# A searched instruction order, engine choice and PSUM bank table for a two-layer SSM and MLP kernel

## The chip, the cores and the metric

The kernel runs as one program on one core of a Trainium2 chip. The core has a matmul engine (TensorE, PE in the profile, with its weight loads shown as PEld), a vector engine (VectorE, DVE), a scalar engine (ScalarE, ACT), a general engine (GpSimd, POOL) and a queue that issues most of the DMA transfers (SyncE, SP). Each of the five works through a list of its own, in order, and waits for the others by semaphores. The metric is device microseconds (us) of one execution, as the median of several; lower is better.

## The reference

An input of 2048 rows of 512 is passed twice through a pair of layers, with residual sums:

```python
x = A_q
x = x + _A_ref(_layernorm(x), A_k, A_v, A_shift_k, A_ssm_k, A_ssm_D)
x = x + _B_ref(_layernorm(x), B_w1, B_b1, B_w2, B_b2)
x = x + _A_ref(_layernorm(x), A_k, A_v, A_shift_k, A_ssm_k, A_ssm_D)
x = x + _B_ref(_layernorm(x), B_w1, B_b1, B_w2, B_b2)
```

`_A_ref(q, k, v, ...)` shifts k by a filter of four taps, multiplies it by v (`kv`), convolves `kv` along the 2048 rows with a filter of 2048 taps per channel (by FFT in the reference), adds `kv * ssm_D` and multiplies the sum y by the normed q. `_B_ref` is a layer norm, a 512 to 1376 matmul with bias and GELU, and a 1376 to 512 matmul with bias. Since k, v and the filters are the same in both passes, y is the same in both, and the kernel computes it once.

## The kernel before

The long convolution is done as a transform in matmuls, in two halves of 1024 rows. The source marks every operation with a stage name (`P.tag`), and the text below uses these names; `_0` and `_1` are the halves:

- `ht`, `h1`, `h2`: the filter is transposed (L540), goes through a first stage of matmuls (L557, 8 tiles of 16 matmuls) and a second (L569, 8 tiles of 16). A tile `t` of the second stage reads two of the 16 pieces of a constant table, `tab_s2` (256 KB each, operations 16 to 31, loaded at L463). `swap` copies the result from SBUF to SBUF in 8 transfers (issued by SP, L453).
- `fir0` to `fir3`: k is transposed (L589), the four-tap filter is a group of 22 matmuls (L614), and DVE multiplies the result by v (L620). Each of these products reads all four pieces of v of its half.
- `x1`, `x2`: the same two stages for kv (L557, L569). In `x2_0` DVE multiplies each result tile by the filter's transform (16 products of 128x1024, line L468).
- `i1`, `i2`: the way back, L674 and L696. Its result is y.

All of these stages evacuate PSUM through one helper, `evac` (L473 when it is ACT, L474 when it is DVE). From `i2_0` on the first half's blocks run: for a block b the stages are `q`b (layer norm of x, then y times it, added to x: `y`b, line L468), `z`b (a second norm, its statistics by L810/L811 on DVE and three small operations L815, L817, L822 or L825 on POOL or DVE, then L835 on ACT or L836 on DVE), a transpose (L887 on PE for the first two, by DMA at L879 for the others), `m1` (L899, one PSUM tile for each of 11 chunks, GELU on ACT at L904) and `m2` (L933, added to x by DVE at L937). The second half's transform (`h2_1` with products on DVE at L767, `fir4` to `fir7`, `p2`, `x1_1`, `x2_1`, `sum`, `i1_1`, `i2_1`) is threaded through the first half's blocks on the same engines; `p2`, `x2_1` and `sum` are DVE operations of 128x2048 at L468.

Nothing of the order is written out in the program's text. `op()` records 1185 operations with what they read and write. `arrange()` then takes three tables. `SEQ` is a permutation of the 1185 numbers, and the list of each engine is `SEQ` cut down to the operations of that engine. `ENGS` holds a letter (a, v, p for ACT, DVE, POOL) for each operation that could run on more than one engine. `BANKS` holds a digit for each PSUM tile, the first of its one or two banks (there are eight); a tile waits until the last user of its banks is through. `sync()` derives the semaphore waits from these lists: `d_N` is the landing of DMA operation N, `s_scalar`, `s_vector` and so on are counts of an engine's finished operations.

```python
self.seq = [self.ops[i] for i in self.SEQ]
choice = iter(self.ENGS)
for t, b in zip(self.tiles, self.BANKS):
    t.base = int(b)
```

Of the kernel before, what the change touches and what calls it, by code (L numbers as in the profile page):

```python
# [36 lines left out]
class Prog:  # L37
# [7 lines left out]
        42, 0, 6, 43, 214, 1, 4, 33, 2, 5, 34, 41, 7, 3, 195, 9, 11, 10, 8, 196, 51, 14, 197, 45, 52, 12, 209, 46, 35,  # L45
        53, 13, 36, 48, 28, 54, 49, 47, 20, 55, 67, 15, 59, 68, 19, 388, 50, 65, 32, 39, 430, 63, 60, 23, 40, 22, 64,
        66, 17, 56, 44, 69, 21, 38, 431, 389, 57, 24, 70, 390, 71, 29, 58, 391, 61, 18, 432, 37, 16, 62, 97, 134, 103,
        215, 392, 27, 104, 433, 98, 101, 26, 99, 136, 102, 105, 393, 31, 106, 100, 111, 72, 25, 114, 30, 108, 115,
        135, 133, 109, 116, 110, 112, 131, 113, 121, 132, 107, 129, 127, 130, 122, 472, 77, 528, 78, 125, 526, 126,
        79, 128, 80, 85, 73, 75, 74, 76, 117, 86, 139, 118, 89, 140, 83, 90, 474, 84, 123, 91, 473, 119, 124, 92, 120,  # L50
        81, 87, 475, 82, 476, 161, 88, 477, 169, 162, 478, 302, 93, 165, 434, 170, 173, 166, 94, 96, 143, 174, 95,
        181, 144, 194, 137, 182, 167, 200, 189, 163, 199, 185, 190, 210, 138, 177, 198, 186, 171, 141, 204, 175, 193,
        157, 178, 201, 159, 164, 142, 191, 187, 158, 155, 179, 147, 301, 183, 156, 153, 294, 184, 148, 220, 188, 176,
        160, 211, 216, 386, 192, 208, 154, 205, 172, 218, 203, 180, 221, 202, 222, 168, 206, 219, 226, 223, 217, 228,
        283, 580, 227, 224, 435, 527, 229, 230, 225, 282, 582, 149, 231, 479, 145, 529, 150, 530, 286, 146, 232, 531,
        234, 233, 240, 212, 532, 482, 235, 394, 581, 436, 151, 241, 395, 290, 238, 437, 295, 152, 396, 236, 438, 287,
        239, 397, 254, 583, 439, 398, 248, 399, 237, 255, 292, 242, 400, 256, 440, 401, 441, 243, 284, 442, 402, 291,
        244, 257, 584, 403, 585, 443, 249, 410, 412, 586, 406, 207, 411, 250, 444, 213, 407, 420, 293, 445, 258, 414,
        424, 387, 413, 422, 425, 259, 408, 421, 452, 288, 466, 409, 480, 418, 453, 416, 467, 483, 448, 417, 481, 456,
        419, 404, 285, 484, 449, 260, 485, 405, 289, 454, 415, 458, 423, 487, 251, 455, 536, 486, 462, 488, 426, 252,  # L60
        489, 457, 490, 463, 261, 427, 533, 491, 262, 459, 450, 494, 446, 253, 428, 447, 537, 495, 460, 451, 464, 429,
        492, 263, 534, 245, 590, 264, 493, 468, 461, 265, 465, 587, 469, 246, 470, 538, 247, 296, 535, 268, 541, 496,
        269, 471, 502, 497, 267, 539, 500, 503, 514, 272, 588, 501, 540, 510, 591, 515, 266, 542, 508, 592, 511, 543,
        589, 512, 270, 509, 544, 634, 498, 513, 273, 516, 298, 499, 545, 506, 517, 297, 504, 546, 635, 518, 593, 505,
        547, 595, 507, 522, 548, 594, 300, 523, 549, 596, 636, 597, 598, 299, 303, 271, 637, 599, 275, 638, 602, 310,
        524, 603, 304, 311, 639, 519, 305, 600, 640, 306, 520, 644, 307, 601, 558, 570, 521, 641, 554, 525, 571, 552,
        559, 689, 566, 568, 567, 645, 550, 278, 555, 556, 564, 557, 279, 562, 569, 560, 563, 610, 551, 276, 604, 611,
        608, 565, 642, 561, 616, 690, 609, 691, 622, 617, 620, 646, 605, 692, 612, 274, 553, 693, 606, 613, 624, 607,
        643, 614, 625, 694, 649, 572, 623, 615, 277, 695, 621, 308, 314, 309, 281, 322, 315, 576, 647, 696, 573, 323,
        280, 699, 320, 697, 316, 321, 648, 700, 318, 698, 574, 701, 317, 650, 702, 577, 651, 652, 319, 575, 312, 704,  # L70
        653, 313, 626, 703, 705, 744, 706, 578, 707, 654, 336, 708, 579, 655, 618, 337, 656, 328, 745, 746, 630, 619,
        657, 338, 329, 324, 627, 709, 747, 330, 748, 711, 749, 631, 710, 325, 339, 750, 340, 712, 332, 326, 632, 333,
        668, 633, 672, 669, 676, 341, 331, 628, 673, 660, 334, 677, 664, 661, 344, 665, 629, 721, 662, 722, 342, 731,
        345, 352, 335, 674, 663, 715, 675, 670, 353, 343, 717, 729, 671, 348, 718, 346, 658, 349, 382, 727, 383, 347,
        725, 659, 385, 713, 716, 384, 733, 714, 350, 719, 732, 730, 723, 751, 678, 354, 666, 680, 667, 351, 679, 720,
        684, 726, 355, 754, 685, 734, 327, 686, 728, 724, 735, 687, 366, 752, 755, 368, 367, 753, 756, 358, 757, 360,
        359, 759, 681, 799, 361, 758, 682, 760, 800, 369, 801, 761, 762, 364, 858, 370, 365, 763, 802, 860, 356, 803,
        855, 764, 371, 362, 861, 862, 765, 804, 736, 363, 766, 856, 805, 767, 737, 357, 857, 863, 859, 683, 739, 864,
        806, 865, 738, 374, 809, 807, 372, 866, 376, 373, 810, 808, 375, 740, 811, 377, 812, 782, 876, 867, 814, 786,
        778, 813, 873, 868, 788, 877, 774, 779, 815, 878, 870, 816, 772, 874, 770, 817, 869, 789, 875, 741, 775, 871,  # L80
# [893 lines left out]
```

## Time and profile before

| | us |
|---|---|
| median of 3 runs (lowest, highest) | 237.92 (237.78, 238.18) |
| the profiled execution's own time | 237.62 |
| its span, first to last instruction | 235.8 |
| PE busy | 223.4 |
| DVE busy | 177.0 |
| ACT busy | 161.7 |
| POOL busy | 55.2 |

The page cuts the span into 40 slices of 5.9 us and gives the busy share of each in tenths. The chain of waits follows the work that ended last back from step to step. The timeline gives start, length, engine, line and, in brackets, idle time ahead of a row with what ended it. A row of the timeline that merges several instructions (x4) reaches from the start of the first to the end of the last. On ACT and DVE an instruction starts about 0.1 us before the one ahead of it has ended, so the step from start to start is a little shorter than the length of one.

### The profile page before, as it was taken

The page shows a single profiled execution, that of the slowest core. Times are in us where ns is not written, and L with a number is a line of the kernel's source. Part 1 is how long each engine was busy: PE and PEld are TensorE (multiplying, and loading weights), DVE is VectorE, ACT ScalarE, POOL GpSimd, SP SyncE. Part 2 cuts the span into 40 slices and gives each one's busy share as a digit, 9 for nine tenths or more (in the row PEclk, how much of TensorE's full clock was granted, in tenths as well). Part 3 has the DMA queues.
Part 4 walks back from the last instruction along what each step waited for, and adds up shares of the span by engine and source line. Part 5 has one row for each costly group of instructions (what it writes and reads, how often), then busy time and mean ns, then how long its engine had stood idle before and what let it go on. Part 6 is the DMA issues. An engine that isn't in the chain of part 4 may idle for free.

```text
span 235.8 us, 6520 instructions
## 1 busy us (share of the span) xinstructions
PE 223.4 (95%) x2765; PEld 146.6 (62%) x2765; DVE 177.0 (75%) x355; ACT 161.7 (69%) x259; POOL 55.2 (23%) x117
## 2 busy tenths in 40 slices
PE   6796887998999999999999999999999999999995
PEld 3785777875968588667967585644444444444453
DVE  0678989999999999989999899385379388705004
ACT  2962999998996789998987995998037403810910
POOL 1550020924222405344002831402020301100000
PEclk9999999999999999999999999999999999999999
DMA  6999879983976930022140203301300140071302
GB/s 210 301 375 386 311 208 282 264 288 70 174 119 177 198 79 0 3 48 45 31 151 6 45 3 69 67 0 22 67 0 4 22 111 0 0 134 47 133 0 92
DMA packets 41113, 26.77 MB, mean 114 GB/s; under 512 B 23702, under 2 KB 33788, under 8 KB 41084
## 3 DMA queue, kind: packets, MB, share of 16 engines
q1 hardware_dynamic: 40786, 26.20, 41.2%
q8 instruction: 22, 0.36, 0.7%
q10 hardware_dynamic: 298, 0.16, 0.3%
q14 instruction: 7, 0.06, 0.1%
HBM read 15.07 MB, written 2.10 MB: 73 GB/s over the span
## 4 chain that ended last, share of the span: by engine, by line
PE 77%; DVE 7%; ACT 6%; SPq 4%; DMA 4%; issue 1%; DVEq 0%
PE ps L899 33%; PE ps L933 32%; ACT ar L473 6%; PE ps L569 4%; DMA ar<-in_A_v_dram 4%; DVE ar L468 4%; SPq L453 3%; PE ps L674 2%; PE ps L696 2%; DVE ar L620 2%; PE ps L557 2%; DVE ar L474 2%; PE ps L922 1%; PE ps L642 1%; SPq L463 0%
## 5 line engine op out<-in xcount | busy, mean ns | idle before, releaser
L904 ACT ACTIVATE ar<-ps,sm 128x256 bf16<-128x256 f32 (+4 forms) x143 | 64.8, 525 | 35.1 <-PE ps L899 34.8
L473 ACT ACTIVATE ar<-ps 128x1024 bf16<-128x1024 f32 (+3 forms) x77 | 71.6, 1003 | 14.7 <-PE ps L557 6.2
L899 PE MATMUL ps<-ar 128*128 128x256 bf16 (+4 forms) x572 | 81.0, 297 | 0.2 <-ACT ar L473 0.2
L933 PE MATMUL ps<-ar 128*128 128x512 bf16 (+1 forms) x341 | 78.3, 379 | 0.0
L899 PEld LDWEIGHTS ps<-ar 128*128 128x128 bf16 (+1 forms) x572 | 52.7, 100 | 26.1 <-ACT ar L473 0.3
L468 DVE TENSOR_TENSOR ar<-ar 128x512 bf16<-128x512 bf16 (+3 forms) x105 | 62.6, 641 | 4.5 <-ACT ar L473 3.0
L933 PEld LDWEIGHTS ps<-ar 128*128 128x128 bf16 (+1 forms) x341 | 32.5, 98 | 36.5 <-ACT ar L904 0.4
L810 DVE BATCH_NORM_STATS2 sm<-ar 128x6 f32<-128x512 bf16 x64 | 42.6, 682 | 0.4
L835 ACT ACTIVATE ar<-ar,sm 128x512 bf16<-128x512 bf16 x38 | 30.2, 823 | 12.6 <-DVE sm L822 10.5
L815 POOL TENSOR_SCALAR sm<-sm 128x2 f32<-128x2 f32 (+2 forms) x22 | 7.6, 347 | 109.0 <-DVE sm L811 108.4
L937 DVE TENSOR_TENSOR ar<-ar,ps 128x512 bf16<-128x512 bf16 x31 | 20.4, 679 | 16.1 <-PE ps L933 16.1
L817 POOL TENSOR_TENSOR sm<-sm 128x2 f32<-128x2 f32 (+2 forms) x26 | 21.2, 814 | 21.8 <-DVE sm L815 19.9
L557 PE MATMUL ps<-ar 128*64 128x128 bf16 x512 | 17.2, 221 | 2.8 <-POOL ar L468 1.2
L569 PE MATMUL ps<-ar 128*128 128x64 bf16 x512 | 18.3, 193 | 1.3 <-ACT ar L473 0.9
L569 PEld LDWEIGHTS ps<-ar 128*128 128x128 bf16 x512 | 16.9, 98 | 3.2 <-ACT ar L473 1.4
L557 PEld LDWEIGHTS ps<-ar 128*64 128x64 bf16 x512 | 14.8, 110 | 5.6 <-ACT ar L473 1.6
L474 DVE CAST ar<-ps 128x1024 bf16<-128x1024 f32 x13 | 15.8, 1220 | 2.4 <-PE ps L569 1.3
L836 DVE TENSOR_SCALAR ar<-ar,sm 128x512 bf16<-128x512 bf16 x26 | 9.9, 406 | 5.1 <-POOL sm L825 5.0
L825 POOL TENSOR_SCALAR sm<-sm 128x1 f32<-128x1 f32 x40 | 13.2, 347 | 1.9
L674 PE MATMUL ps<-ar 64*128 64x64 bf16 (+1 forms) x384 | 12.6, 203 | 0.5 <-ACT ar L473 0.3
L674 PEld LDWEIGHTS ps<-ar 64*128 64x128 bf16 (+1 forms) x384 | 11.9, 114 | 1.9 <-ACT ar L473 1.2
L767 DVE SCALAR_TENSOR_TENSOR ar<-ar,sm,ps 128x512 bf16<-128x512 bf16 x16 | 10.9, 744 | 0.4 <-PE ps L569 0.4
(42 smaller groups left out, 90.3 us busy)
## 6 DMA issues: line engine op xcount, KB each, us to landing
ar<-tab_s SPq DMA_DIRECT2D x16, 256.0 KB, 9.0
ar<-ar SPq DMA_DIRECT2D x16, 256.0 KB, 4.5
ar<-in_A_ssm_k_dram SPq DMA_DIRECT2D x8, 256.0 KB, 7.1
ar<-in_A_q_dram SPq DMA_DIRECT2D x8, 256.0 KB, 4.9
ar<-in_A_v_dram SPq DMA_DIRECT2D x8, 256.0 KB, 6.8
out_dram<-ar SPq DMA_DIRECT2D x7, 256.0 KB, 2.5
ar<-in_B_w_dram SPq DMA_DIRECT2D x4, 344.0 KB, 5.6
ar<-in_B_w_dram SPq DMA_DIRECT2D x5, 256.0 KB, 4.1
```

Of the source, the lines that this page charges most:

```text
L468: return P.op(eng, lambda e: e.tensor_tensor(o, a, b, op), dur, reads=[a, b] + list(more), writes=[o])
L473: return e.activation(dst, src(), AF.Copy)
L474: return e.tensor_copy(dst, src())
L557: r = e.matmul(Q(tl, 64 * ri, 64, i * 128, [1, 128]), w, m, start=True, stop=True)
L569: r = e.matmul(Q(tl, 0, 128, i // 8 * 512 + i % 8 * 4, [32, 16], [1, 4]), w, m, start=True, stop=True)
L674: r = e.matmul(Q(tl, 0, 128, i, *([32, 16], [1, 4]) if split else ([1, 128],)), w, m, start=n == 0, stop=n == 1)
L810: P.op(DVE, lambda e, sj=sj, x=x: e.bn_stats(sj, x), 600.0, reads=[x], writes=[sj])
L817: P.op(POOL, lambda e: e.tensor_tensor(r, v, hf, ALU.pow), 420.0 + 149.0 * n, reads=[v, hf], writes=[r])
L835: return e.activation(o, x, AF.Identity, bias=u, scale=r)
L899: r = e.matmul(Q(tl, 0, rows, 0, [1, w]), a, m, start=dk == 0, stop=dk == 3)
L904: P.op(ACT, lambda e, dst=dst, tl=tl, rows=rows, bias=bias, w=w: e.activation(dst, Q(tl, 0, rows, 0, [1, w]), AF.Gelu_apprx_tanh, bias=bia ...
L933: r = e.matmul(Q(tl, 0, 128, 0, [1, 512]), ins[fc][0], ins[fc][1], start=fc == 0, stop=fc == 10)
```

## The change

The three tables are replaced as a whole. No operation is added or taken away, no operation changes its size, and the program around the tables is word for word the same. A few entries of each:

```diff
     SEQ = (
-        42, 0, 6, 43, 214, 1, 4, 33, 2, 5, 34, 41, 7, 3, 195, 9, 11, 10, 8, 196, 51, 14, 197, 45, 52, 12, 209, 46, 35,
+        6, 44, 0, 41, 33, 2, 4, 1, 5, 34, 214, 7, 3, 195, 8, 13, 11, 10, 215, 51, 9, 29, 45, 197, 52, 20, 53, 15, 48,
...
     ENGS = (
-            "avapapvpaavvaavaavaaaaavvvvapvppvavvavaavaavvaaaaaaaavaaaaaaaaavaavaaaaaapvpvaaaaaaaaaaaaaaaaaaaaaaaaaaa"
+            "apvvvvvpavaaaavvvvaaaaaavaavvvvpvaaaavaavaavvaaaaaaavvaaaaaaaaavaavaaaaaapppvaaaaaaaaaaaaaaaaaaaaaaaaaaa"
...
     BANKS = (
-            "45704306202464200000627236026646246464226006402420624644066042640262264600644466440666002624266260062444"
+            "01162540642622644266440453046220460662226460224226040240260620602401064460626446404464404602426446424242"
```

By the letters, DVE has 370 operations where it had 355, six have left ACT and nine have left POOL. Three places are shown in full.

The first place is SP's list at the start, where the first transfers are issued. Both lists begin with the four pieces of the filter and one of q (256 KB each); these five rows are left out. `in_A_k`, `in_A_v` and `in_A_q` are pieces of the first half's inputs, `tab_s2` pieces of the table of the second stage. Before:

```order
L453 DMA ar<-in_A_k_dram 128x1024 x4
L453 DMA ar<-in_A_q_dram 128x1024
L453 DMA ar<-in_A_v_dram 128x1024
L453 DMA ar<-in_A_q_dram 128x1024
L453 DMA ar<-in_A_v_dram 128x1024
L453 DMA ar<-in_B_b2_dram 1x512
L453 DMA ar<-in_A_v_dram 128x1024
L463 DMA ar<-tab_s2 128x1024 x2
L453 DMA ar<-in_A_v_dram 128x1024
L463 DMA ar<-tab_s2 128x1024
L463 DMA ar<-tab_small 128x256
L463 DMA ar<-tab_s2 128x1024 x8
```

And now:

```order
L453 DMA ar<-in_A_k_dram 128x1024
L453 DMA ar<-in_A_v_dram 128x1024
L453 DMA ar<-in_A_k_dram 128x1024 x3
L463 DMA ar<-tab_s2 128x1024
L453 DMA ar<-in_A_q_dram 128x1024
L463 DMA ar<-tab_s2 128x1024
L453 DMA ar<-in_A_v_dram 128x1024 x3
L463 DMA ar<-tab_s2 128x1024 x4
L453 DMA ar<-in_B_b2_dram 1x512
L463 DMA ar<-tab_s2 128x1024
L453 DMA ar<-in_A_q_dram 128x1024
L463 DMA ar<-tab_s2 128x1024 x5
```

The last piece of v was the 17th transfer of 256 KB and is the 16th; one piece of q has moved behind it. Among the table's pieces, 20 and 21 were the 16th and the 22nd transfer and are the 13th and the 26th; 28 was the 15th and is the 23rd; 29 was the 24th and is the 11th.

The second place is the stretch in which `x1_0` (L557) and `h2_0` (L569) start, on PE and on DVE. On PE, from the third tile of `x1_0`, before:

```order
L557 MATMUL ps<-ar 64x128 [waits s_vector]
L557 MATMUL ps<-ar 64x128 x15
L557 MATMUL ps<-ar 64x128 [waits s_scalar]
L557 MATMUL ps<-ar 64x128 x15
L569 MATMUL ps<-ar 128x16x4 [waits d_20,d_21,s_vector]
L569 MATMUL ps<-ar 128x16x4 x15
L557 MATMUL ps<-ar 64x128 [waits s_scalar]
L557 MATMUL ps<-ar 64x128 x15
L569 MATMUL ps<-ar 128x16x4 [waits d_23,d_22,s_scalar]
L569 MATMUL ps<-ar 128x16x4 x15
L569 MATMUL ps<-ar 128x16x4 [waits d_28,d_29,s_scalar]
L569 MATMUL ps<-ar 128x16x4 x15
```

And now, from the same tile:

```order
L557 MATMUL ps<-ar 64x128 [waits s_vector]
L557 MATMUL ps<-ar 64x128 x15
L569 MATMUL ps<-ar 128x16x4 [waits d_29,d_28,s_scalar]
L569 MATMUL ps<-ar 128x16x4 x15
L557 MATMUL ps<-ar 64x128 [waits s_scalar]
L557 MATMUL ps<-ar 64x128 x15
L569 MATMUL ps<-ar 128x16x4 [waits d_20,d_21,s_scalar]
L569 MATMUL ps<-ar 128x16x4 x15
L557 MATMUL ps<-ar 64x128 [waits s_vector]
L557 MATMUL ps<-ar 64x128 x15
L569 MATMUL ps<-ar 128x16x4 [waits d_17,d_16,s_vector]
L569 MATMUL ps<-ar 128x16x4 x15
```

The first tile of `h2_0` is now the one that needs the table's pieces 28 and 29, and it stands one tile of `x1_0` earlier. Ahead of these rows, the first two tiles of `x1_0` now stand before the last of the four L614 groups; all four groups were ahead of them. On DVE, after the four products L620, before:

```order
L474 CAST ar<-ps 128x1024
L810 BN_STATS sm<-ar 128x6 x3
L474 CAST ar<-ps 128x1024
L474 CAST ar<-ps 128x2x16x32
L474 CAST ar<-ps 128x1024
L810 BN_STATS sm<-ar 128x6
L811 BN_AGGR sm<-sm 128x2
L474 CAST ar<-ps 128x1024
L811 BN_AGGR sm<-sm 128x2
L474 CAST ar<-ps 128x2x16x32
L632 COPY ar<-ar 128x3
L474 CAST ar<-ps 128x2x16x32
```

And now:

```order
L603 COPY ar<-ar 128x3
L810 BN_STATS sm<-ar 128x6
L474 CAST ar<-ps 128x1024
L474 CAST ar<-ps 128x2x16x32 x2
L811 BN_AGGR sm<-sm 128x2 x2
L815 TENSOR_SCALAR sm<-sm 128x2
L822 SCALAR_TENSOR_TENSOR sm<-sm 128x2
L474 CAST ar<-ps 128x1024
L474 CAST ar<-ps 128x2x16x32
L474 COPY ar<-ps 128x8x16x8
L468 TENSOR_TENSOR ar<-ar 128x2x8x64 x3
L474 CAST ar<-ps 128x2x16x32
```

Seven evacuations (CAST) have become six. The seventh has gone to ACT, which now has 31 evacuations from the first of `x1_0` to the last of `i1_0` where it had 30.

The third place is DVE where `i2_0` ends and the first block's second norm (`z0`) begins. Before:

```order
L468 TENSOR_TENSOR ar<-ar 128x512
L811 BN_AGGR sm<-sm 128x2
L468 TENSOR_TENSOR ar<-ar 128x512 x3
L632 COPY ar<-ar 128x3
L810 BN_STATS sm<-ar 128x6 x2
L811 BN_AGGR sm<-sm 128x2 x3
L767 SCALAR_TENSOR_TENSOR ar<-ar,sm,ps 128x16x32 x8
```

And now:

```order
L468 TENSOR_TENSOR ar<-ar 128x512 x3
L810 BN_STATS sm<-ar 128x6
L468 TENSOR_TENSOR ar<-ar 128x512
L811 BN_AGGR sm<-sm 128x2
L810 BN_STATS sm<-ar 128x6
L811 BN_AGGR sm<-sm 128x2
L822 SCALAR_TENSOR_TENSOR sm<-sm 128x1
L767 SCALAR_TENSOR_TENSOR ar<-ar,sm,ps 128x16x32 x6
```

The two L468 of block 0 now stand together, its statistics (the first L810 and L811) come ahead of those of block 1, and the last small operation of `z0` (L822, on POOL as L825 before) is DVE's, ahead of the L767 of `h2_1`. The PSUM tile of the first L767 pair and that of the `z0` transpose (L887) now share bank 2.

9 lines of the change are left out of this document (5 added, 4 removed), and 108 rows, old and new, of the table SEQ.

## The prediction

> **What bounds the kernel now.** I read the page first: the busy shares, the slices, the shares of the chain. Then came the windows, to find where TensorE stops, and then the timelines of TensorE, ACT and DVE there. The page:
>
> ```profile
> span 235.8 us, 6520 instructions
> ...
> PE 223.4 (95%) x2765; PEld 146.6 (62%) x2765; DVE 177.0 (75%) x355; ACT 161.7 (69%) x259; POOL 55.2 (23%) x117
> ...
> PE   6796887998999999999999999999999999999995
> ...
> DVE  0678989999999999989999899385379388705004
> ACT  2962999998996789998987995998037403810910
> ...
> PEclk9999999999999999999999999999999999999999
> ...
> PE 77%; DVE 7%; ACT 6%; SPq 4%; DMA 4%; issue 1%; DVEq 0%
> ```
>
> PE is below 9 only in the first ten slices (59 us) and the last. Its clock is full throughout. So a reorder of the same matmuls can gain only from PE's idle time: 235.8 - 223.4 = 12.4 us, nearly all ahead of 59 us. Behind that PE is full, and a change there can only open gaps. Two windows show it (start:end, length, then busy time of PE, PEld, DVE, ACT, POOL, clock, DMA share and GB/s):
>
> ```profile
> 20.00:30.00 10.00, 8.49 (x222) 7.25 (x222) 9.68 (x10) 7.43 (x8) 0.00 (x0) 1.00 0.89 327
> ...
> 60.00:80.00 20.00, 20.00 (x330) 14.90 (x331) 19.97 (x44) 16.42 (x42) 4.36 (x13) 1.00 0.85 178
> ```
>
> From 60 to 80 DVE is as full as PE: a term that delays DVE there delays PE soon after. The time is therefore set by when PE's unbroken run begins, near the first m1 (L899, 59.11), plus any new gap. What leads up to it, on ACT (start, length, in brackets the idle time ahead and its releaser):
>
> ```profile
> 21.62 1.02 ACT L473 ACTIVATE ar<-ps 128x1024 bf16<-128x1024 f32 x1 [4.79 <-PE ps L557]
> 23.02 3.99 ACT L473 ACTIVATE ar<-ps 128x1024 bf16<-128x1024 f32 x4 [0.37 <-PE ps L557]
> 27.29 1.94 ACT L473 ACTIVATE ar<-ps 128x1024 bf16<-128x1024 f32 x2 [0.28 <-PE ps L569]
> 29.41 19.62 ACT L473 ACTIVATE ar<-ps 128x1024 bf16<-128x1024 bf16 x21 [0.18 <-PE ps L540]
> 49.52 7.76 ACT L473 ACTIVATE ar<-ps 128x1024 bf16<-128x1024 f32 x9 [0.49 <-PE ps L674]
> 57.15 0.81 ACT L835 ACTIVATE ar<-ar,sm 128x512 bf16<-128x512 bf16 x1
> ```
>
> From 21.6 to 57 ACT evacuates PSUM almost without a stop, 19.62/21 = 0.93 each, and PE waits for its tiles. In this stretch the evacuation work of ACT (beside DVE's) sets the pace, and ahead of it the arrival of v, which the chain shows (start, length):
>
> ```profile
> 10.05 8.55 DMA ar<-in_A_v_dram
> 18.68 2.36 DVE ar L620 x2
> ```
>
> **The change, part by part.** The first part is SP's start order. The last v piece of the first half lands at 10.05 + 8.55 = 18.60 and the first product L620 starts 0.08 later. It moves from the 17th to the 16th transfer. The rate is the last column here:
>
> ```profile
> 10.00:20.00 10.00, 6.88 (x164) 6.16 (x166) 7.25 (x12) 5.16 (x6) 4.66 (x13) 1.00 1.03 364
> ```
>
> 262144 bytes at 364 GB/s are 0.72 us, so the first L620 goes from 18.68 to about 17.95 (T1, -0.7; ends 0 and -0.72, and I take the second because the queue is full at 1.03).
>
> The first two tiles of `x1_0` now stand ahead of the fourth L614 group. On PE:
>
> ```profile
> 19.96 1.05 PE L614 MATMUL ps<-ar 64*128 64x256 bf16 x22 [1.71 <-DVE ar L620]
> 20.95 1.08 PE L557 MATMUL ps<-ar 128*64 128x128 bf16 x32
> ...
> 23.47 0.64 PE L569 MATMUL ps<-ar 128*128 128x64 bf16 x16
> ...
> 25.23 0.64 PE L569 MATMUL ps<-ar 128*128 128x64 bf16 x16 [0.50 <-ACT ar L473]
> ```
>
> The first tile is ready one product (2.36/2 = 1.2) and 0.64 for the tile behind 17.95, so ACT's first evacuation moves from 21.62 to about 19.85 (T2, -1.77 with T1 in it).
>
> The gain meets the table. The first `h2_0` tile now needs piece 28, which was the 15th transfer of 256 KB and is the 23rd; at 0.72 to 0.80 us each (364 and 327 GB/s) behind the 16th at 17.9 it lands at 22.9 to 23.4. PE could begin at about 22.2, and everything of PE stands behind it. I take 23.3, because the second rate is that of the window it falls in; ACT then idles some 0.65. The second tile needs piece 21, the 26th transfer, at 25.1 to 25.8, where PE is ready at 24.3 to 25.0: I take 25.3 and 0.95 of idle (T3, +1.6 together; ends 0.7 and 2.2).
>
> Then ACT does 31 evacuations where it did 30, since DVE does six L474 CAST where it did seven (T4, +0.93; ends 0.93 and, should that tile be one of the halves of 128x512, the 0.81 of the row at 57.15). Before: from 21.62 to the end of the last `i1_0` evacuation at 49.52 + 0.93 x 2, about 51.4, are 29.8 us, of which 30 x 0.93 = 27.9 are work and 1.9 idle. After: of the 1.9 the 0.18 and 0.49 of the rows stay, 1.6 are T3, and 0.6 lies between the first tiles, where the L614 group of 1.05 now stands; 2.9 in all. 19.85 + 31 x 0.93 + 2.9 = 51.55 (T4 and T3 against T2). So -1.77 + 0.93 + 1.0 = +0.1 at the end of `i1_0`: the earlier start is used up.
>
> The next part is the first block's norm. It sets when the L887 transpose and so the first m1 can start:
>
> ```profile
> 58.02 0.40 PE L887 MATMUL ps<-ar 128*128 128x128 bf16 x4 [0.75 <-ACT ar L835]
> 59.11 0.84 PE L899 MATMUL ps<-ar 128*128 128x128 bf16 x12 [0.22 <-ACT ar L473]
> ```
>
> ```profile
> 52.97 0.42 DVE L468 TENSOR_TENSOR ar<-ar 128x512 bf16<-128x512 bf16 x1
> 55.66 0.30 DVE L811 BATCH_NORM_AGGREGATE sm<-sm 128x2 f32<-128x6 f32 x3
> 56.38 4.04 DVE L767 SCALAR_TENSOR_TENSOR ar<-ar,sm,ps 128x512 bf16<-128x512 bf16 x6 [0.41 <-PE ps L569]
> 55.93 0.19 POOL L815 TENSOR_SCALAR sm<-sm 128x1 f32<-128x1 f32 x1 [3.59 <-DVE sm L811]
> 56.20 0.55 POOL L817 TENSOR_TENSOR sm<-sm 128x1 f32<-128x1 f32 x1
> 56.85 0.26 POOL L825 TENSOR_SCALAR sm<-sm 128x1 f32<-128x1 f32 x1
> ```
>
> With block 0's two L468 and its statistics first, the aggregate ends at about 55.4 instead of 55.96, although the first L468 starts 0.1 to 0.2 later. Two small POOL operations follow, 0.27 + 0.65 from start to start. The third is DVE's: 0.16 taken (0.10, one of three L811 rows, to the 0.26 of POOL). The norm starts at 56.6 instead of 57.15 (T5, -0.55). But the L887 transpose now shares bank 2 with the first L767 pair (4.04/6 = 0.67 each), and its start comes out at 57.95, not 57.5. That covers nearly all of T5: the first m1 moves from 59.11 to 59.05 (-0.06). If bank 2 is freed without a wait, it is -0.5; if the pair starts 0.3 late, +0.3.
>
> The opening stretch runs from the first m1 to the first m2 (L933), PE first and then ACT:
>
> ```profile
> 60.06 3.03 PE L899 MATMUL ps<-ar 128*128 128x128 bf16 x48
> ...
> 63.86 0.64 PE L569 MATMUL ps<-ar 128*128 128x64 bf16 x16
> 64.34 0.39 PE L899 MATMUL ps<-ar 128*128 128x128 bf16 x4
> 64.56 1.67 PE L933 MATMUL ps<-ar 128*128 128x512 bf16 x7
> ```
>
> ```profile
> 60.73 3.59 ACT L904 ACTIVATE ar<-ps,sm 128x128 bf16<-128x128 f32 x13
> ```
>
> Twelve m1 chunks (48 matmuls) take PE 3.03, 0.25 each, where an unhindered one takes 0.22 (64.34 to 64.56), and a GELU takes ACT 3.59/13 = 0.28: PE runs here at the pace at which GELU empties its tiles. Now one chunk (0.22) and one L569 group (0.48, 63.86 to 64.34) stand behind the first m2 and no longer in this stretch, while the GELUs in it are as many. So the 5.45 of the stretch do not shrink by the 0.70 that moved but by about 0.4, as ACT's pace allows, and the other 0.3 is a new stop of PE (T6, +0.3; ends 0, if ACT begins its GELUs as much earlier, and 0.7, if it does not let the stretch shrink at all).
>
> The rest moves at no cost, by these covers. The work of DVE up to the last `sum` is one L836 shorter by the list, and PE is full meanwhile. The L468 products of `x2_1` are the same in number. The last transposed k piece is now issued behind a `swap` and lands, by my walk along SP's list, some 0.5 ahead of the L642 group that reads it: the thinnest cover, and if it goes, PE waits for a few tenths. The norms of the later blocks keep the lead over their transposes that they had, apart from block 6, below. BANKS elsewhere costs nothing while ACT and DVE empty tiles as early as now. The tail is as it was.
>
> Sum against the profiled execution's 237.62 (span 235.8): -0.06 (T1 to T5) + 0.3 (T6) = +0.24, 237.86. The median of the runs shown, 237.92, stands 0.30 above that execution; so 238.2 for the median, +0.1%. A measurement of this kernel can tell some 0.2%, 0.48 us, from no change; by that the forecast is no change.
>
> **The rivals.** A, faster. T3 is not paid, because the table lands earlier than 0.72 to 0.80 per piece, or PE reaches it later than I have it; and bank 2 is free when L887 comes. Then the 0.7 of T1 or the 0.5 of T5 lives to the first m1 and T6 stays at 0.1: 59.11 becomes about 58.4, and the time 237.92 - 0.9 = 237.0. For it: PE's idle time ahead of 59 us is the only thing there is to gain and the change works there. Against it: the 31st evacuation, which is certain by the letters.
>
> B, slower, in block 6's norm. POOL's small operations beside DVE's two-input products:
>
> ```profile
> 38.05 8.51 DVE L468 TENSOR_TENSOR ar<-ar 128x1024 bf16<-128x1024 bf16 x14
> 41.53 5.41 POOL L632 COPY ar<-ar 128x3 bf16<-128x3 bf16 x2 [7.36 <-PE ps L557]
> ...
> 101.31 0.19 POOL L815 TENSOR_SCALAR sm<-sm 128x2 f32<-128x2 f32 x1 [0.49 <-DVE sm L811]
> 102.39 0.50 POOL L825 TENSOR_SCALAR sm<-sm 128x1 f32<-128x1 f32 x2
> 103.98 1.20 DVE L468 TENSOR_TENSOR ar<-ar 128x2048 bf16<-128x2048 bf16 x1
> ```
>
> Two copies of three elements, which cannot be long by themselves, took 5.41 us beside an unbroken row of L468 and ended with it. In block 6 the statistics on POOL ended at 102.9, 1.1 ahead of the run of long L468 (1.20 each). In the new list those start at about 103.1 to 103.7, and POOL's at the earliest end at 102.9 to 103.0. If POOL comes too late by more than the 0.1 to 0.7 that is left, its last operation waits for a gap in the products; the L835 that heads ACT's list then holds back an evacuation of `x2_1` behind it, and PE stops for one product, 1.1 to 1.2: 238.2 + 1.2 = 239.4. [...]
>
> C, slower, at the start: T3 is larger, because the pieces 28 and 21 land later than I have it. It decides from about 0.5 each beyond 23.3 and 25.3, which is 1.4 transfers of 0.72. ACT has no slack to catch up (0.67 us of idle in all behind 29.4), so it comes through as +0.6 to +1.0 at the first m1: about 238.9.
>
> **How the numbers follow.** The forecast (237.4 to 238.4) has 0.36. A has 0.28, since its condition needs only one of two terms to be off by half a us. C has 0.21, because two waits of PE on transfers that are moved eight and four places back are sure to exist in the list and only their length is open. B has 0.15, as it needs a miss of a few tenths in one place of many. A is the faster side, B and C the slower one: 0.28, 0.36, 0.36. The range reaches over A's 237.0 with its largest sum (T1 and T5 both, 236.7) and over C and B to 239.6.
>
> **What the profile would show.** T1: the first L620 at about 17.95. T2 and T3: ACT's first evacuation of `x1_0` near 19.85, and then two L569 groups on PE that a DMA released, near 23.3 and 25.3. T4: 31 ACT evacuations in unbroken rows up to about 51.6. T5: the L835 near 56.6, and the L887 behind it released by DVE's L767, not by ACT. T6: PE waiting for L904 between the first m1 and the first L933, which comes at about 64.1. B: a POOL row of more than 1 us near 103. PE full from there to 233.5. The prediction is wrong if PE's run of full slices starts before 58.5 or after 59.6, or if a slice behind 65 us falls below 9.

## The result and the profile after

| | median us | of the kernel before, beside it | ratio, 95% interval |
|---|---|---|---|
| changed kernel | 241.65 (240.80 to 243.13, 6 runs) | 238.01 (237.49 to 238.68, 6 runs) | 1.0158 (1.0128 to 1.0188) |

The change costs 1.6%, some 3.7 us. The forecast was no change (238.2), with a range that ended at 239.6. In some series below single executions ran longer at a lower granted clock; the ratios leave out those that are over 1.5% above the fastest of their kernel.

The page of the changed kernel, with the same lines as the prediction showed of the kernel before:

```profile
span 239.5 us, 6513 instructions
...
PE 226.0 (94%) x2765; PEld 147.2 (61%) x2765; DVE 181.7 (76%) x370; ACT 158.0 (66%) x253; POOL 52.0 (22%) x104
...
PE   7987888999996999999999999999999999999994
...
DVE  0889779999999899989999989694569397723013
...
PEclk9999999999999999999999999999999999999999
```

The first ten slices look like those before. The new thing is the 6 in the 13th slice (72 to 78 us), in a stretch where PE had been full: the prediction's own sign of being wrong, a slice behind 65 us below 9. The timeline of PE there, and around the two points from which the prediction counted (start, length, and the idle time ahead with its releaser):

```profile
57.62 0.40 PE L887 MATMUL ps<-ar 128*128 128x128 bf16 x4 [0.32 <-DVE ar L767]
...
58.71 1.07 PE L899 MATMUL ps<-ar 128*128 128x128 bf16 x16
...
63.85 1.03 PE L933 MATMUL ps<-ar 128*128 128x512 bf16 x4
...
76.31 1.12 PE L642 MATMUL ps<-ar 32*128 32x128 bf16 x88 [1.84 <-DMA ar<-in_A_k_dram]
```

The first m1 (L899) comes at 58.71 instead of 59.11, a gain of 0.40. Then PE stops 1.84 us for a piece of k. The chain of waits shows that piece, from its issue at 70.30 to its landing 5.96 later:

```profile
70.30 5.96 DMA ar<-in_A_k_dram
```

In 2.0 of these 5.96 us the DMA engines moved next to nothing. The window from 73.5 to 75.5 has 15 GB/s in its last column, and the view of DMA in the same window names, beside the queue of the kernel's transfers, one packet of 0.02 MB (16 KB) of an instruction queue:

```profile
73.50:75.50 2.00, 0.97 (x9) 0.65 (x7) 2.00 (x8) 1.55 (x4) 0.00 (x0) 1.00 0.20 15
```

```profile
q8 instruction: 1, 0.02, 3.0%
```

PE was ready for the piece at 74.47 (76.31 less 1.84). Without these 2.0 us it would have landed near 74.3, an estimate, and PE would hardly have stopped. What held the transfers there is not shown.

A second, smaller stop stands at 143, where the chain goes through block 8's second norm (z8):

```profile
139.12 1.61 POOL sm L815
...
140.80 0.71 POOL sm L817
...
141.54 0.17 DVE sm L822
...
141.74 0.81 ACT ar L835
142.55 0.37 ACT ar L904
...
142.97 1.05 PE ps L899 x8
```

Each of these waits for the one above it. ACT had all its GELUs behind that L835 and stood idle for 0.85 until 141.74; PE waited for the GELU behind it.

At the end the last product on DVE (L926) starts at 236.39 and the span ends at 239.5, 2.8 us after that product's end; before, it started at 233.45 and the span ended at 235.8, 2.1 after. So 0.75 of the loss lies behind the last product. The timeline of the tail has 33 L933 in a row, then all of L922, and the four last transfers of SP in one piece; the second fence is the last product of the kernel before:

```profile
226.61 7.30 PE L933 MATMUL ps<-ar 128*128 128x512 bf16 x33
...
234.66 2.65 SPq L453 DMA_DIRECT2D out_dram<-ar  x4
...
236.39 0.29 DVE L926 TENSOR_TENSOR ar<-ar,ps 128x128 bf16<-128x128 bf16 x1 [0.33 <-PE ps L922]
```

```profile
233.45 0.29 DVE L926 TENSOR_TENSOR ar<-ar,ps 128x128 bf16<-128x128 bf16 x1 [0.33 <-PE ps L922]
```

The ledger of the two profiled executions, whose spans differ by 3.7:

| place | us |
|---|---|
| up to the first m1 | -0.40 |
| first m1 to first m2: 5.14 instead of 5.45, with 0.70 of work moved out | +0.39 |
| stop at L642: 1.84 idle, and up to 0.1 because such a group elsewhere starts a little before the one ahead has ended (0.07 for the one at 82.45) | +1.9 to 2.0 |
| z8: the L899 at 142.97 and the L933 at 144.03 start 0.47 and 0.18 later behind the matmul ahead than such matmuls do elsewhere (0.31 and 0.01 after its end, elsewhere 0.16 and 0.17 before it) | +0.65 |
| behind the last product | +0.75 |
| left over, not traced to a place | +0.3 to 0.4 |

### The profile page after: what moved, and what is told of

It reads as the page before. It is cut to its first block, busy times and chain, and to the rows that moved or that the text cites. A ratio compares the mean times of both kernels' runs of the same rounds, so it can differ in the third digit from the quotient of the medians.

```text
span 239.5 us, 6513 instructions
## 1 busy us (share of the span) xinstructions
PE 226.0 (94%) x2765; PEld 147.2 (61%) x2765; DVE 181.7 (76%) x370; ACT 158.0 (66%) x253; POOL 52.0 (22%) x104
## 4 chain that ended last, share of the span: by engine, by line
PE 69%; ACT 11%; DVE 9%; DMA 5%; SPq 2%; issue 2%; POOL 2%; DVEq 0%; POOLq 0%
PE ps L933 28%; PE ps L899 27%; ACT ar L473 8%; PE ps L557 3%; DVE ar L468 3%; PE ps L569 3%; DMA ar<-in_A_k_dram 2%; DMA ar<-ar 2%; PE ps L674 2%; DVE ar L767 2%; ACT ar L904 2%; PE ps L511 1%; PE ps L540 1%; SPq L453 1%; PE ps L922 1%
## 5 line engine op out<-in xcount | busy, mean ns | idle before, releaser
L904 ACT ACTIVATE ar<-ps,sm 128x256 bf16<-128x256 f32 (+5 forms) x143 | 65.7, 523 | 50.1 <-PE ps L899 49.7
L899 PE MATMUL ps<-ar 128*128 128x256 bf16 (+5 forms) x572 | 81.5, 297 | 0.3 <-ACT ar L904 0.3
L473 ACT ACTIVATE ar<-ps 128x1024 bf16<-128x1024 f32 (+3 forms) x76 | 70.6, 1003 | 14.0 <-PE ps L557 4.5
L933 PE MATMUL ps<-ar 128*128 128x512 bf16 (+1 forms) x341 | 77.9, 379 | 0.0
L899 PEld LDWEIGHTS ps<-ar 128*128 128x128 bf16 (+1 forms) x572 | 52.5, 100 | 27.1 <-ACT ar L904 0.6
L468 DVE TENSOR_TENSOR ar<-ar 128x512 bf16<-128x512 bf16 (+3 forms) x106 | 62.8, 636 | 1.9 <-ACT ar L835 0.8
L933 PEld LDWEIGHTS ps<-ar 128*128 128x128 bf16 (+1 forms) x341 | 32.4, 98 | 37.0 <-ACT ar L904 0.5
L810 DVE BATCH_NORM_STATS2 sm<-ar 128x6 f32<-128x512 bf16 x64 | 42.4, 682 | 0.4
L817 POOL TENSOR_TENSOR sm<-sm 128x2 f32<-128x2 f32 (+2 forms) x26 | 22.8, 876 | 57.3 <-DVE sm L815 55.8
L835 ACT ACTIVATE ar<-ar,sm 128x512 bf16<-128x512 bf16 x33 | 26.1, 811 | 4.0 <-POOL sm L825 2.0
L815 POOL TENSOR_SCALAR sm<-sm 128x2 f32<-128x2 f32 (+2 forms) x18 | 6.7, 375 | 69.8 <-DVE sm L811 69.5
L557 PE MATMUL ps<-ar 128*64 128x128 bf16 x512 | 18.4, 221 | 3.3 <-ACT ar L473 2.1
L569 PE MATMUL ps<-ar 128*128 128x64 bf16 x512 | 18.9, 193 | 1.6 <-DVE ar L474 0.8
L569 PEld LDWEIGHTS ps<-ar 128*128 128x128 bf16 x512 | 16.9, 98 | 4.4 <-ACT ar L473 1.6
L557 PEld LDWEIGHTS ps<-ar 128*64 128x64 bf16 x512 | 15.0, 110 | 6.9 <-ACT ar L473 3.5
L825 POOL TENSOR_SCALAR sm<-sm 128x1 f32<-128x1 f32 x33 | 14.9, 467 | 1.6
L836 DVE TENSOR_SCALAR ar<-ar,sm 128x512 bf16<-128x512 bf16 x31 | 11.5, 407 | 2.4 <-POOL sm L825 2.2
L767 DVE SCALAR_TENSOR_TENSOR ar<-ar,sm,ps 128x512 bf16<-128x512 bf16 x16 | 11.0, 739 | 0.3 <-PE ps L569 0.3
```

The costliest lines, as they stand in the source:

```text
L468: return P.op(eng, lambda e: e.tensor_tensor(o, a, b, op), dur, reads=[a, b] + list(more), writes=[o])
L473: return e.activation(dst, src(), AF.Copy)
L557: r = e.matmul(Q(tl, 64 * ri, 64, i * 128, [1, 128]), w, m, start=True, stop=True)
L569: r = e.matmul(Q(tl, 0, 128, i // 8 * 512 + i % 8 * 4, [32, 16], [1, 4]), w, m, start=True, stop=True)
L810: P.op(DVE, lambda e, sj=sj, x=x: e.bn_stats(sj, x), 600.0, reads=[x], writes=[sj])
L817: P.op(POOL, lambda e: e.tensor_tensor(r, v, hf, ALU.pow), 420.0 + 149.0 * n, reads=[v, hf], writes=[r])
```

## The experiments

All compare with the kernel before, which ran on the same chip between the others; its medians were 237.86 (first set: the piece of k first, and by two places, the y9 products, one output transfer), 237.91 (second set: the changed kernel again, the tail's order, the three repairs, the fault in the kernel before) and 237.66 (third set: all others). The numbers in the diffs are the operations' numbers.

### The piece of k issued first

```diff
     SEQ = (
...
-        480, 424, 407, 483, 418, 292, 423, 481, 454, 409, 456, 484, 425, 452, 485, 455, 466, 453, 414, 282, 467, 487,
+        480, 424, 407, 483, 418, 292, 423, 481, 454, 409, 456, 484, 425, 452, 485, 455, 466, 453, 414, 282, 290, 467, 487,
...
-        460, 459, 246, 428, 461, 533, 247, 468, 283, 590, 534, 269, 469, 535, 587, 290, 265, 470, 429, 496, 266, 471,
+        460, 459, 246, 428, 461, 533, 247, 468, 283, 590, 534, 269, 469, 535, 587, 265, 470, 429, 496, 266, 471,
```

> The changed kernel with one transfer moved: the last transposed piece of k (L779) is issued right behind the v piece of 63.12, ahead of the two z2 transposes, the second v piece and the first swap copy. Theory K: the 1.84 us that PE stops at 76.31 for this piece is the largest term of the loss and comes through whole. Then the piece is issued near 64.8 and lands before 71, that row of PE has no idle time, and the time is 241.65 - 1.9 = about 239.7. Rival D: DVE, 19.32 of 20 us busy from 60 to 80, would have stopped PE a little later anyway, so that less than half comes back: 240.7 or more.

Measured: 239.12 (238.85 to 239.85, 12 runs), ratio 1.0057 (1.0034 to 1.0081). The timelines of SP and of PE:

```profile
64.45 1.20 SPq L779 DMA_TRANSPOSE ar<-in_A_k_dram  x1
```

```profile
71.00 3.22 PE L899 MATMUL ps<-ar 128*128 128x256 bf16 x28
74.16 1.11 PE L642 MATMUL ps<-ar 32*128 32x128 bf16 x88
```

The stop is gone and its time comes back whole: theory K holds, D is out. One transfer's place in SP's list was 1.8 us (against the second measurement of the changed kernel, 240.93) to 2.5 us (against the first, 241.65), the largest part of the loss.

### The piece of k moved by two places

```diff
     SEQ = (
...
-        460, 459, 246, 428, 461, 533, 247, 468, 283, 590, 534, 269, 469, 535, 587, 290, 265, 470, 429, 496, 266, 471,
+        460, 459, 246, 428, 461, 533, 247, 468, 290, 283, 590, 534, 269, 469, 535, 587, 265, 470, 429, 496, 266, 471,
```

> The same transfer moved less far: it stays behind the two z2 transposes and is put ahead of the second v piece and the first swap copy, so it is issued at about 69.0 and not at 70.3. If its 6 us to landing came from the 256 KB copies put in flight just ahead of it (theory F), it now lands in about 3 us, near 72 to 73, ahead of the 74.3 at which PE wants it, and the time is 239.7 as well. If the place behind the z2 transposes, which wait for a norm, is what counts (rival Z), it lands near 75 and PE still stops for some 0.7: 240.4.

Measured: 240.52 (238.12 to 241.69, 6 runs), ratio 1.0111 (1.0070 to 1.0152). The median is that of rival Z (240.4), not that of theory F (239.7). In the profiled execution, the shortest of the six, the piece was issued at 67.83 with nothing of 256 KB just ahead, and L642 did not wait for it:

```profile
67.83 1.26 SPq L779 DMA_TRANSPOSE ar<-in_A_k_dram  x1
69.14 0.58 SPq L453 DMA_DIRECT2D ar<-in_A_v_dram  x1
69.76 6.42 SPq L453 DMA_DIRECT2D ar<-ar  x7
```

```profile
73.23 1.11 PE L642 MATMUL ps<-ar 32*128 32x128 bf16 x88
```

The piece, here and then in the changed kernel, by the view of DMA issues (the last number is us from issue to landing):

```profile
ar<-in_A_k_dram SPq DMA_TRANSPOSE x1, 2.9
```

```profile
ar<-in_A_k_dram SPq DMA_TRANSPOSE x1, 6.0
```

That one execution agrees with theory F: the piece landed in 2.9 us with the two 256 KB transfers behind it and not ahead. But its short time is not the edit's alone, since it stood at the first m1 (57.53) 1.2 us ahead of the changed kernel already. The other executions reach up to 241.7 and were not profiled, so whether the piece came late in them stays open, and theory F is not shown. As a repair the place is not safe; the one further forward, with a spread of 1.0 us, is.

### The same fault put into the kernel before

```diff
     SEQ = (
...
-        234, 233, 240, 212, 532, 482, 235, 394, 581, 436, 151, 241, 395, 290, 238, 437, 295, 152, 396, 236, 438, 287,
+        234, 233, 240, 212, 532, 482, 235, 394, 581, 436, 151, 241, 395, 238, 437, 295, 152, 396, 236, 438, 287,
...
-        492, 263, 534, 245, 590, 264, 493, 468, 461, 265, 465, 587, 469, 246, 470, 538, 247, 296, 535, 268, 541, 496,
+        492, 263, 534, 245, 590, 264, 493, 290, 468, 461, 265, 465, 587, 469, 246, 470, 538, 247, 296, 535, 268, 541, 496,
```

> The kernel before with one transfer moved the other way: the second of its transposed pieces of k goes behind the two z2 transposes, so it is issued near 69.7 and not at 54.1. Theory K: the place in SP's list alone makes the stop. The piece lands at about 72.5 to 74, PE wants it at 71.24, and PE stops for 1.3 to 2.8: 237.9 + 2.0 = about 239.9. Rival: the matmuls behind it have slack enough to close the gap, or it lands by 71.3: within 0.5 of 237.9.

Measured: 241.86 (241.09 to 245.02, 6 runs), ratio 1.0152 (1.0112 to 1.0193). Theory K holds in direction, and the size was too small by half. The chain has the landing at 69.47 + 4.15 = 73.62, inside the forecast:

```profile
69.47 4.15 DMA ar<-in_A_k_dram
```

No 256 KB transfer was issued just ahead of it here, only the two z2 transposes, as in the execution with 2.9. So what stands just ahead does not by itself set the time to landing. From 72 to 73 the DMA engines moved 8 GB/s, a shorter stretch of the kind seen in the changed kernel. PE's timeline and the windows (start:end, length, busy PE, PEld, DVE, ACT, POOL, clock, DMA share, GB/s) show what was missed:

```profile
73.67 1.74 PE L642 MATMUL ps<-ar 32*128 32x128 bf16 x88 [2.66 <-DMA ar<-in_A_k_dram]
75.34 5.93 PE L899 MATMUL ps<-ar 128*128 128x256 bf16 x44
```

```profile
72.00:74.00 2.00, 0.33 (x28) 0.34 (x32) 2.00 (x6) 0.00 (x0) 0.00 (x0) 0.98 0.39 90
74.00:76.00 2.00, 2.00 (x80) 1.74 (x68) 2.00 (x6) 0.00 (x0) 1.50 (x4) 0.50 1.00 285
76.00:78.00 2.00, 2.00 (x14) 1.53 (x13) 2.00 (x7) 1.14 (x3) 0.09 (x1) 0.67 1.02 288
```

The kernel before had, for the same 88 and 44 matmuls:

```profile
71.24 1.11 PE L642 MATMUL ps<-ar 32*128 32x128 bf16 x88
72.29 4.98 PE L899 MATMUL ps<-ar 128*128 128x256 bf16 x44
```

So the stop of 2.66 is followed by some 3.4 us at a granted clock of 0.50 (an estimate from the clocks of these three windows, 0.98, 0.50 and 0.67: 0.08 + 2.0 + 1.32), in which the same matmuls took 0.63 + 0.95 = 1.6 us longer. Together that is 4.2; 3.9 arrive at the end. That clock is not a fixed part of this price: five of the six executions have a mean granted clock of 0.993 or less, and the sixth, at 1.000, took 241.09, still 3.2 above the kernel before. The kernel before has such a clock too, in 3 of its 17 executions in this set (238.81 to 239.91).

### The y9 products moved behind block 8's statistics

```diff
     SEQ = (
...
-        876, 873, 772, 815, 870, 816, 375, 774, 874, 868, 817, 788, 769, 871, 773, 784, 875, 775, 855, 770, 818, 869,
+        876, 873, 772, 815, 870, 816, 375, 774, 817, 788, 769, 773, 784, 775, 855, 770, 818, 874, 868, 871, 875, 869,
```

> The changed kernel with the four y9 products (L468, two inputs in SBUF) of DVE moved behind the z8 operation L822, which waits for POOL. Theory P: POOL's L815 of block 8 took 1.60 us because these products kept it out; alone it takes 0.19. Then L815 is 0.2 long, L822 comes about 1.4 earlier, ACT does not wait 0.85 for the norm at 141.74, and the stops of PE at 142.97 and 144.03 (0.47 + 0.18 behind what the matmuls need) go: 241.65 - 0.65 = 241.0. Rival: L815 is long here for another reason, or PE's stops have another cause: 241.65 and the same rows.

Measured: 240.17 (239.83 to 240.42, 6 runs), ratio 1.0086 (1.0061 to 1.0112). On POOL, with the changed kernel first and this one second:

```profile
139.12 1.60 POOL L815 TENSOR_SCALAR sm<-sm 128x2 f32<-128x2 f32 x1 [2.10 <-DVE sm L811]
```

```profile
138.90 0.26 POOL L815 TENSOR_SCALAR sm<-sm 128x2 f32<-128x2 f32 x1 [2.10 <-DVE sm L811]
```

And what ran on DVE while the first of these L815 took 1.60:

```profile
139.25 1.42 DVE L468 TENSOR_TENSOR ar<-ar 128x512 bf16<-128x512 bf16 x4
141.54 0.16 DVE L822 SCALAR_TENSOR_TENSOR sm<-sm 128x2 f32<-128x2 f32 x1 [0.87 <-POOL sm L817]
```

Theory P holds. L815 lasted until the four products had ended (139.25 + 1.42 = 140.67), and without them it takes 0.26. All four went by before it ended, at 140.72, although it had started 0.13 ahead of the first of them (139.12 and 139.25). By what means they held it is not shown. PE's stops at 143 are gone. The time fell by 0.76 against the changed kernel in the second set, where 0.65 was expected; the two intervals overlap, so that the cause rests on the rows rather than on this difference.

### The tail, twice

```diff
     SEQ = (
...
-        1164, 1174, 1168, 1165, 1176, 1169, 1170, 1182, 1177, 1178, 1179, 1183, 1175, 1180, 1184, 1181)
+        1164, 1174, 1168, 1165, 1176, 1169, 1175, 1170, 1182, 1177, 1178, 1179, 1183, 1180, 1184, 1181)
```

> The changed kernel with one output transfer moved: the 128 KB piece whose data is ready at 233.33 and which SP issued at 235.97, behind two others, is issued first. Theory T: the last transfer was issued at 236.88, 0.8 after its data, because SP's list held it, and the outputs crowd; it is now issued at about 236.1, and the end comes 0.7 earlier: 240.95. Rival: the crowd itself sets the end (four transfers within 2.7 us after the last products whatever their order), and the time stays within 0.3 of 241.65.

Measured: 240.59 (240.23 to 240.86, 6 runs), ratio 1.0103 (1.0077 to 1.0128). That is 0.34 below the changed kernel as measured in the second set, and the intervals overlap. In the trace the last product ends at 236.18 and the span at 238.8: 2.6 behind it, 0.2 less. Nearer to the rival: the crowd stays.

The changed kernel was then run once more, as the line for the second set:

> The changed kernel once more, on the chip and beside the runs of the three others, as the line from which their differences are taken. Expected by every theory: the ratio of the first measurement, 1.016, within some 0.3%, so 241.4 to 242.0 beside 237.9; and the 1.84 us stop of PE at the L642 near 76.3 again.

Measured: 240.93 (240.38 to 241.72, 6 runs), ratio 1.0117 (1.0081 to 1.0153), 0.7 us less than at first, with the same stop at L642 (1.73 us). So the loss lies between 3.0 and 3.7 us, and single effects of 0.3 us are at the edge of what these runs tell.

```diff
     SEQ = (
...
-        1140, 1143, 1146, 1141, 1160, 1147, 1153, 1158, 1157, 1166, 1161, 1159, 1167, 1171, 1162, 1172, 1163, 1173,
-        1164, 1174, 1168, 1165, 1176, 1169, 1170, 1182, 1177, 1178, 1179, 1183, 1175, 1180, 1184, 1181)
+        1140, 1143, 1146, 1141, 1160, 1147, 1153, 1158, 1157, 1166, 1161, 1159, 1167, 1162, 1163, 1171, 1172, 1164,
+        1168, 1165, 1169, 1170, 1176, 1177, 1178, 1173, 1174, 1175, 1182, 1183, 1184, 1179, 1180, 1181)
...
     BANKS = (
...
-            "75023474606232527101645746762733073404277054331432770434742350102446107233756734416")
+            "75023474606232527101645746762733073404277054331432770434742350102446107233756734016")
```

> The changed kernel with the last m2 products of PE in an order like that before (two of the three groups end first, the 256-wide L922 before the third), one PSUM tile moved to bank 0, and the outputs issued as they get ready. Moving one transfer alone had shortened the stretch from the last product's end to the last landing only from 2.35 to 2.10, where it was 1.29 before. Theory T: the stretch is long because four outputs are issued within 2.6 us at the end; spread as before it falls to about 1.3 to 1.5, and the time is 241.65 - 1.0 = 240.65. Rival: what is gained there is lost to PE waiting for GELU in the new order: within 0.3 of 241.65.

Measured: 240.63 (240.17 to 241.37, 6 runs), ratio 1.0104 (1.0069 to 1.0140): 0.3 below the line, not 1.0. In the trace the span ends 2.6 behind the last product, where it was 2.8 in the changed kernel and 2.1 in the one before, so most of the crowd stayed; the rest of theory T is not borne out. (The 1.29 of the expectation counts SP's transfers only. The last landing of the kernel before is that of ACT's queue, 1.53 behind its last product, so less was there to gain than 1.0.) A likely reason that the outputs still crowd: the third group's sum is ready at 236.03 only, since its last matmuls now stand behind the first L922.

### The three repairs together

The diffs of the first, the fourth and the last of the runs above, in one kernel.

> The changed kernel with three repairs at once: the piece of k first, the y9 products behind L822, the tail in the other order. If the loss is the sum of these three terms (theory S): 241.65 - 2.0 - 0.65 - 1.0 = 238.0, level with before. If they hide each other, or a fourth term of the same size is there (rival): 239.5 or more.

Measured: 238.70 (237.15 to 239.19, 12 runs), ratio 1.0010 (0.9985 to 1.0035). Theory S holds but for a small rest: of the loss of 3.0 to 3.7 us some 0.2 stays by this ratio. It was run again as a line for the next set:

> The kernel with the three repairs once more, as the line beside which the next one is read: the same ratio, 1.001 within 0.3%, so 237.5 to 238.8 beside 237.9.

Measured: 238.38 (237.52 to 238.74, 12 runs), ratio 1.0023 (1.0002 to 1.0045). By this one some 0.5 stays, and the interval just leaves out no change. Together the three bring 2.2 to 2.6 against the second measurement of the changed kernel, and singly 1.8 + 0.76 + 0.3 = 2.9.

### The front alone, and the front with the opening

```diff
     SEQ = (
-        (the order before, whole)
+        (the changed order ahead of operation 152, near 53 us; then the order before, without these)
...
```

ENGS and BANKS are taken for each operation and tile from the same side.

> The new order, engines and banks for everything up to the third h1_1 tile that stands inside i2_0 (near 53 us), and the order before for all that follows, block 0's second norm among it. This is the front alone (T1 to T4). In the profile of the changed kernel the first L696 stood at 51.35 where it was 51.52. Theory: the front is worth 0.2 at most, so 237.9 - 0.2 = 237.7. Rival: the front costs something that the later parts of the changed kernel hide: 238.4 or more.

Measured: 237.85 (237.05 to 240.87, 12 runs), ratio 1.0007 (0.9991 to 1.0024): no difference, to within the interval of some 0.6 us. This agrees with the prediction's sum of T1 to T4 (+0.1): what the front gains by v and by the early `x1_0` is used up.

```diff
     SEQ = (
-        (the order before, whole)
+        (the changed order ahead of operation 461, near 68 us, with 290 behind 282; then the order before, without these)
...
```

> The new order, engines and banks up to the middle of the opening stretch (near 68 us), with the last piece of k issued first, and the order before for all that follows. Beside the front alone it has the new z0 order (T5) and the new opening (T6). The profiles gave -0.4 at the first m1 and +0.5 up to 70, so the theory is 237.9 + 0.1 = 238.0, with the first m1 near 58.7. Rival: the opening costs more when what follows is the old order: 238.6 or more.

Measured: 238.83 (238.04 to 239.68, 9 runs), ratio 1.0048 (1.0028 to 1.0068). This one doesn't tell the theories apart, because there is a stop near the seam that neither whole kernel has:

```profile
68.61 0.60 PE L933 MATMUL ps<-ar 128*128 128x512 bf16 x2
69.99 2.55 PE L933 MATMUL ps<-ar 128*128 128x512 bf16 x11 [0.78 <-DVE ar L937]
```

Of the 1.2 above the kernel before, 0.4 are left without these 0.78, between the two forecasts. Whether the new opening is worth its place stays open.

### One norm taken from ACT in the opening

On the kernel with the three repairs:

```diff
     ENGS = (
...
-            "avppapvaappvppaavvvvppaavpaavpaappaapvaappaappvavpaappaappaappvvppaapvaappavvavvvvvvvvavavpvvavvpvvvvvvp"
+            "avppapvaappvppvavvvvppaavpaavpaappaapvaappaappvavpaappaappaappvvppaapvaappavvavvvvvvvvavavpvvavvpvvvvvvp"
```

> The same with one letter changed: the second block's norm, 0.80 on ACT ahead of the first GELU (L835), goes to DVE, 0.41 between the L767. Theory G (T6): ACT's GELUs set PE's pace in the opening stretch, and 0.80 less ahead of them shortens it: PE goes from the first m1 to the first m2 in 4.7 to 4.9 where it took 5.14, and the time falls by 0.3 against all_three_again. Rival: DVE is as full there (19.3 of 20 us), so the L767 behind it come 0.41 later and the time is the same or up to 0.4 longer.

Measured: 238.38 (237.50 to 239.06, 12 runs), ratio 1.0030 (1.0013 to 1.0046), the same as beside it. Theory G falls in this form. In PE's timeline the first m1 and first m2 stand at 58.77 and 64.12; without the edit at 58.67 and 64.02, 5.35 both times. ACT did wait:

```profile
57.05 1.66 ACT L473 ACTIVATE ar<-ps 128x1024 bf16<-128x1024 f32 x2
59.20 1.07 ACT L904 ACTIVATE ar<-ps,sm 128x128 bf16<-128x128 f32 x3 [0.49 <-PE ps L899]
60.16 0.60 ACT L473 ACTIVATE ar<-ps 128x512 bf16<-128x512 bf16 x1
60.64 3.28 ACT L904 ACTIVATE ar<-ps,sm 128x128 bf16<-128x128 f32 x12
```

The 0.80 that the norm left free became 0.49 of idle time ahead of the first GELU, which cannot start before the first m1. The norm ahead of the GELUs had thus been in time. That the run of GELUs itself, 3.28/12 = 0.27 each, sets the pace behind it is argued from these rows; no run changes it.

## Why the prediction was wrong

**The step that failed** is the sentence on the last transposed piece of k among what moves at no cost: "lands, by my walk along SP's list, some 0.5 ahead of the L642 group that reads it: the thinnest cover, and if it goes, PE waits for a few tenths". PE was ready for that group at 74.47, so a cover of 0.5 means a landing near 74.0, 3.7 us after the issue at 70.30; it took 5.96, and the price was 1.84 us, not tenths. The term that was named as the thinnest had got no chance and no rival of its own, and the range ended below the time. Moving the one transfer in both kernels, each in its direction, shows that its place is the cause of the stop. Why it took 5.96 there is not shown. Two things go with it in the traces: the two transfers of 256 KB issued just ahead (theory F), and the 2.0 us from 73.5 to 75.5 in which the DMA engines moved 15 GB/s. The second alone is more than the 1.84, and all five profiles with the piece in this place have such a stretch.

**Rival B happened, in another place.** POOL's L815 took 1.60 beside DVE's two-input products, and 0.26 without them; then L835 waited at the head of ACT's list, then PE waited for what stood behind L835: a GELU here, where the prediction had an evacuation. It was put at block 6, where POOL's operations ended at 104.78 in time, while at block 8 it cost 0.65 where 1.1 to 1.2 had been the price. The prediction had worked it out for the long products of `x2_1` only, not for the short ones of the second half's blocks.

**"The tail is as it was"** was wrong by 0.75: the last m2 groups end together now. Two edits took back only about 0.3 of it.

**T1 to T4 were right in sum, in part by luck.** The first L620 started at 17.70 (17.95 forecast) and the first `x1_0` evacuation at 19.64 (19.85). But the last piece of v landed at 16.6 (issued at 8.95, 7.7 to landing), not at 17.9: DVE was busy without a stop from 16.62 with other work of its list, and that set the 17.70:

```profile
16.62 0.50 DVE L603 COPY ar<-ar 128x3 bf16<-128x3 bf16 x2
17.03 0.68 DVE L810 BATCH_NORM_STATS2 sm<-ar 128x6 f32<-128x512 bf16 x1
...
17.70 3.47 DVE L620 TENSOR_TENSOR ar<-ps,ar 128x1024 bf16<-128x1024 f32 x3
```

The transfers behind that piece came earlier too, so T3 was not paid: piece 28 landed at 21.5 (issued at 12.59, 8.9 to landing) where 23.3 was taken, and neither of the two L569 groups waited for a DMA. ACT's rows give what stood in its place:

```profile
19.64 2.15 ACT L473 ACTIVATE ar<-ps 128x1024 bf16<-128x1024 f32 x2 [0.23 <-PE ps L557]
22.33 1.94 ACT L473 ACTIVATE ar<-ps 128x1024 bf16<-128x1024 f32 x2 [0.53 <-PE ps L557]
25.00 2.85 ACT L473 ACTIVATE ar<-ps 128x1024 bf16<-128x1024 f32 x3 [0.73 <-PE ps L569]
28.10 6.52 ACT L473 ACTIVATE ar<-ps 128x1024 bf16<-128x1024 f32 x7 [0.24 <-PE ps L557]
34.79 14.77 ACT L473 ACTIVATE ar<-ps 128x1024 bf16<-128x1024 f32 x16 [0.17 <-PE ps L569]
50.27 5.87 ACT L473 ACTIVATE ar<-ps 128x1024 bf16<-128x1024 f32 x7 [0.70 <-PE ps L674]
56.27 0.81 ACT L835 ACTIVATE ar<-ar,sm 128x512 bf16<-128x512 bf16 x1
```

These are the 31 evacuations up to the last of `i1_0` (2 + 2 + 3 + 7 + 16 + 1), with 0.53 + 0.73 + 0.24 + 0.17 + 0.70 = 2.4 us of idle time among them, where 2.9 was forecast: ACT waits for PE's tiles, with or without the table. The front alone measured as no difference.

**T5 was there and larger**: L835 at 56.27 (56.6 forecast), L887 at 57.62, released by L767 as forecast but 0.3 earlier, so -0.40 at the first m1 and not -0.06. **T6 was right in size**: 5.14 from the first m1 to the first m2 (5.1 forecast), +0.39 (+0.3 forecast); the norm taken from ACT did not shorten it, so what sets the pace is argued only. The two cancel. Of rivals A and C, A's first condition was met, and its gain was spent in the same stretch.

## What to carry to other kernels

When an order is changed, the dear thing is not the work that moves but the transfer whose slack is smallest: for each load that a full engine reads, compare its landing with the time at which it is read, and give a thin cover a rival of its own. A cover of 0.5 us is none here: the eight loads of this kind took from 2.8 to 6.0 us to land in the changed kernel. The stop of 1.84 us gave 1.8 to 2.5 us back when it was taken away, and behind the stop of 2.66 came some 3.4 us at a clock of 0.50 as well. On the queue the fix is cheap: the piece needed nothing that was late, and one place in a list was worth 2 us of 240.

## What the runs showed of the hardware that was not expected

After 2.66 us without a matmul, the granted clock was 0.50 in the next window of 2 us and 0.67 in the one behind it, while it stayed at 1.00 behind the stop of 1.84 us in the changed kernel:

```profile
76.00:78.00 2.00, 1.69 (x94) 1.60 (x95) 1.71 (x4) 0.00 (x0) 1.21 (x3) 1.00 1.17 285
```

The length of the stop does not decide it alone: the profiled execution of the front alone, with a mean granted clock of 0.993, fell to 0.50 (window 34 to 36) with no stop of PE longer than 1.69 us in the ten us ahead of it.

The time from issue to landing of one transposing load of k (128 KB), by what was issued just ahead of it in the same queue:

| just ahead | where | us to landing |
|---|---|---|
| two 128 KB transposes | the piece moved by two places | 2.9 |
| two 128 KB transposes | the fault in the kernel before | 4.15 |
| one 256 KB load | the piece first, alone, with the three repairs (twice), with one norm moved, and in the front with the opening | 3.7 to 4.0 |
| a 256 KB load and a 256 KB copy, within 1.3 us | the changed kernel (twice), and with the y9 products or the tail changed | 5.6 to 6.0 |

In the last row all five profiles have some 2 us in which the DMA engines moved 15 to 27 GB/s, and in these 2 us one 16 KB packet of the instruction queue. Such a packet came in the changed kernel between 24 and 26 too, while the DMA engines moved 393 GB/s; so the packet alone does not stop them. No run moves it, and the cause of the stretch stays open.
